# Moving the x loads to GpSimd's queue in a spectral filter with an MLP behind it, without zero fill, and with divided last stores

## The chip, the cores and the metric

The kernel runs on one core of a Trainium2 chip. The metric is the device time of one execution in microseconds (us); lower is better. Three runs of the kernel before gave a median of 1433.49 us (1433.35 to 1434.29).

A core has five engines with an instruction queue each: TensorE (PE in the profile; its weight loads are PEld), VectorE (DVE), ScalarE (ACT), GpSimd (POOL) and SyncE (SP). Transfers between the main memory and the on-chip memory are issued from the queues of SP, ACT and POOL and carried out by 16 DMA engines. Every queue works in order: an instruction that waits holds up all that stand behind it on that queue.

## What is computed

The reference, cut to what matters:

```python
X = np.fft.rfft(x, axis=1)                    # x: 4 sequences of 3008 points, 256 channels
Yr = Xr @ w_r - Xi @ w_i + b_r                # complex 256 x 256 mix of the channels
Yi = Xr @ w_i + Xi @ w_r + b_i
Yr = np.sign(Yr) * np.maximum(np.abs(Yr) - 0.01, 0.0)   # the same for Yi
y = np.fft.irfft(Y, n=x.shape[1], axis=1)
h = y.reshape(12032, 256) @ w_in              # w_in: 256 x 2048
out = (h * (1.0 / (1.0 + np.exp(-h)))) @ w_out   # w_out: 2048 x 256
```

## The kernel before

The transform of a sequence (3008 = 47 x 64 points) is a chain of four matrix stages. The first stage, s1 (L166), multiplies x by the table c1. For it a sequence is laid out in 94 rows (NP, two for each of 47) and cut into eight pieces g = 0 to 7 of 1024 columns, so one piece is 94 rows of 4 KB, 376 KB. A piece is loaded by x_load (L143), multiplied in two halves of 512 columns, copied out of PSUM by ScalarE (L184), and stored as 96 rows to a scratch tensor in main memory (L187, 384 KB). For the first sequence (b = 0), pieces 0 to 3 go through PE as plain float32 (L183); pieces 4 to 7 (S1_SPLIT) are first split on VectorE into a high and a low part (cast L179, subtraction L180) and multiplied as three float32r products (s1_product, L162 to L164). Behind the first stage the scratch is read back by pairs of residues (u_load, L229 to L233), twelve pairs u for each sequence: second stage s2 (L236), channel mix and shrinking (mix, L254), third stage i1 (L361), stored to a second scratch. The last stage (i2) runs by blocks of 512 rows and feeds the MLP (mlp1, split_g, mlp2), which runs over ticks (block, hidden slice) and takes the largest part of the time. The transforms of the later sequences are put between the MLP's ticks.

The order of the work is written out by hand (the part under `tc.manual_schedule()`, from L553); each engine and each queue follows that order. What stands around the change:

- At the start POOL clears the tile `zero` (L561) and VectorE clears rows 64 to 127 of seven x buffers (x_pre, L562 to L563). SP loads c1 as 128 rows, of which the last 34 are zeros (L564). Then x_ahead is called seven times (L565 to L566), which issues the loads of pieces 0 to 6 of the first sequence; they go on SP's queue, all other x loads on POOL's (L149). ScalarE and POOL make the high and the low part of c1 (L568, L569). PE runs warming multiplications on `zero` (L577, L578).
- Then come a load of the second stage's first table on SP (t2_load) and the first stage's loop (L643), s1(0, g) for g = 0 to 7, whose stores are issued on SP. After s1(0, 0) and s1(0, 1) another x_ahead each loads piece 7 and the second sequence's piece 0, into the buffers of pieces 0 and 1, on POOL.
- Behind the loop: two weight loads, u_load of the pairs 0, 1 and 2 and the bias on SP, the second sequence's piece 0 through the first stage, four more warming multiplications (L654), and the steps u_step(0, u) (L657), within which the MLP's weights are loaded and split, and seven more x loads are issued.
- At the very end four stores of the last 256 output rows remain: of 68, 60, 34 and 94 rows of 1 KB, by the rows of the transform's layout in which they lie. They are issued by the last loop (L755, L756), the third (k = 2) on POOL and the others on SP. The program's closing line, L776, waits for all transfers and drains the engines.

Of the kernel before, what the change touches and what calls it, by code (L numbers as in the profile page):

```python
# [16 lines left out]

# The sequence of S = 47 * 64 points, t = n1 + 64 n2, f = r + 47 k.
S, D, DFF, NB = 3008, 256, 2048, 4
RR, KK = 47, 64  # L20
NR = 24                 # residues r = 0..23; the others are their conjugates
NU = NR // 2            # pairs of residues
NJ = 32                 # n1 = 32 h + j; row 32 p + j with p = 2 n2 + h
NP = 94
# [4 lines left out]
W_PLAN = [(1, 1), (1, 1), (1, 0), (2, 1), (1, 1), (1, 0), (1, 1), (3, 1), (0, 0), (1, 0), (1, 1), (2, 0), (1, 0)]  # L29
# The first sequence's pieces that are multiplied as float32r parts.  # L30
S1_SPLIT = (4, 5, 6, 7)
# Where the first two sequences' pieces go: of seven buffers.
X_BUFS = [0, 1, 2, 3, 4, 5, 6, 0, 1, 2, 3, 4, 5, 2, 1, 0]
# [3 lines left out]
def dft_tables():  # L37
    """The transforms' tables: of the shapes alone."""
    n1 = np.arange(KK)
    n2 = np.arange(RR)  # L40
    r = np.arange(NR)
    k = np.arange(KK)

    def trig(num, den):
        num = np.mod(num, den)
        c, s = np.cos(2 * np.pi * num / den), np.sin(2 * np.pi * num / den)
        s = np.where(2 * num % den == 0, 0.0, s)
        return c, s

    # first stage: rows p = 2 n2 + h, columns m = 4 r + 2 ri + h  # L50
    c, s = trig(np.outer(n2, r), RR)
    c1 = np.zeros((RR, 2, NR, 2, 2))
    c4 = np.zeros((NR, 2, 2, RR, 2))
    for h in range(2):
        c1[:, h, :, 0, h] = c
        c1[:, h, :, 1, h] = -s
        c4[:, 0, h, :, h] = c.T
        c4[:, 1, h, :, h] = -s.T
    c1[:, :, 0, 1, :] = 0.0
    c4[0, 1] = 0.0  # L60
    # second stage, by residue: rows (ri, n1), columns (ri, k)
    f = r[:, None] + RR * k[None, :]
    flip = np.where(2 * f > S, -1.0, 1.0)
    c, s = trig(n1[None, :, None] * f[:, None, :], S)
    c2 = np.zeros((2, KK, NR, 2, KK))
    fl = flip[None, :, :]
    ct, st = c.transpose(1, 0, 2), s.transpose(1, 0, 2)
    c2[0, :, :, 0, :] = ct
    c2[1, :, :, 0, :] = st
    c2[0, :, :, 1, :] = -st * fl  # L70
    c2[1, :, :, 1, :] = ct * fl
    # and back: rows (ri, k), columns (ri, n1)
    fc = np.where(2 * f > S, S - f, f)
    wt = np.where((fc == 0) | (2 * fc == S), 1.0, 2.0) / S
    wt[0, KK // 2 + 1:] = 0.0
    c3 = np.zeros((2, KK, NR, 2, KK))
    ck, sk = c.transpose(2, 0, 1), s.transpose(2, 0, 1)
    w_, f_ = wt.T[:, :, None], flip.T[:, :, None]
    c3[0, :, :, 0, :] = w_ * ck
    c3[1, :, :, 0, :] = -w_ * f_ * sk  # L80
    c3[0, :, :, 1, :] = w_ * sk
    c3[1, :, :, 1, :] = w_ * f_ * ck
    c3[:, :, 0, 1, :] = 0.0
    c3 = c3.reshape(128, NR * 128).astype(np.float32)
    bits = c3.view(np.uint32).astype(np.uint64)
    bits = ((bits + 0x7FF + ((bits >> 12) & 1)) & 0xFFFFF000).astype(np.uint32)
    c3h = bits.view(np.float32)
    c3l = c3 - c3h
    return {
        "c1": np.pad(c1.reshape(NP, 96), ((0, 128 - NP), (0, 0))).astype(np.float32),  # L90
        "c2": c2.reshape(128, NR * 128).astype(np.float32),
        "c3": np.stack([c3h.reshape(128, NU, 256), c3l.reshape(128, NU, 256)], axis=2).reshape(128, NU * 512),
        "c4": c4.reshape(96, NP).astype(np.float32),
    }
# [3 lines left out]
def spectral_mlp_kernel(ctx: ExitStack, tc: tile.TileContext, x, w_r, w_i, b_r, b_i, w_in, w_out, c1, c2, c3, c4, out):  # L98
    nc = tc.nc
# [20 lines left out]
    def bank(name):  # L120
        """A PSUM bank for a transform; the MLP's are free before it starts."""
        tag, bufs = "d", 2
        if state["prologue"]:
            state["d"] = (state["d"] + 1) % 4
            tag, bufs = (("d", 2), ("acc", 4), ("h", 2), ("acc", 4))[state["d"]]
        return ps.tile([128, 512], F32, tag=tag, bufs=bufs, name=name)
# [3 lines left out]
    def store(dst, src, late=False):  # L130
        """A late store goes out when its data is there and what is urgent is on its way."""
        if late or not state["prologue"]:
            stores.append((dst, src))
        else:
            nc.scalar.dma_start(out=dst, in_=src)
# [5 lines left out]

    # ---- the sequence's transform, residues of the frequency first
    def x_load(b, g):  # L143
        if b < 2:
            t = x_pre[X_BUFS[8 * b + g]]
        else:
            t = x_sb[g % 2]
        v = x[b].rearrange("(p j) d -> p (j d)", j=NJ)
        (nc.sync if b == 0 and g < 7 else nc.gpsimd).dma_start(out=t[:NP, :], in_=v[:, g * 4 * D:(g + 1) * 4 * D])  # L149
        return t  # L150
# [11 lines left out]
    def s1_product(p, hl):  # L162
        for n, (m, k) in enumerate(((0, 0), (0, 1), (1, 0))):
            nc.tensor.matmul(out=p[:96, :], lhsT=c1_hl[m], rhs=hl[k], start=(n == 0), stop=(n == 2))  # L164

    def s1(b, g, late=False):  # L166
# [6 lines left out]
        for i in range(2):  # L173
            p = bank("s1")
            h = t[:, i * 512:(i + 1) * 512]
            if b == 0 and g in S1_SPLIT:
                k, w, n = ("x", 768, 2) if (2 * g + i) % 5 > 2 else ("g", 512, 3)
                hl = [sb.tile([128, w], F32R, tag=k + q, bufs=n, name="sx")[:, :512] for q in "hl"]
                nc.vector.tensor_copy(out=hl[0], in_=h)  # L179
                nc.vector.tensor_sub(hl[1], h, hl[0])  # L180
                s1_product(p, hl)
            else:
                nc.tensor.matmul(out=p[:96, :], lhsT=c1_sb, rhs=h, start=True, stop=True)  # L183
            nc.scalar.copy(o[:, i * 512:(i + 1) * 512], p[:96, :])  # L184
# [6 lines left out]
    def s1_split(b, g, i):  # L191
        t = x_t[b, g][:, i * 512:(i + 1) * 512]
        sx = sb.tile([128, 2, 512], F32R, tag="sx", bufs=1, name="sx")
        nc.scalar.copy(sx[:, 0, :], t)
        nc.vector.tensor_sub(sx[:, 1, :], t, sx[:, 0, :])
        x_t[b, g, i] = sx
# [77 lines left out]

    # The mix in three products instead of four, rows (r, f):
    # (Xr + Xi) w_r - Xi (w_r + w_i) and (Xr + Xi) w_r + Xr (w_i - w_r).
    def mix3_weights():
# [106 lines left out]
    def pieces(c0, n):  # L384
        """Runs of columns (b, j, p) in order: offset, b, j, p0, length."""
        c = c0
# [20 lines left out]
    def i2_columns(p, o, e, b, j, p0, m):  # L407
        """Row j's points p0 .. p0 + m, turned, to p's columns from o on."""
        q = (j % 4) * D + e * 128
# [4 lines left out]
    def i2(i, e):  # L414
        """Block i's rows that lie wholly in it, for one half of d."""
        c0, n = BLOCKS[i]
# [11 lines left out]
    def i2_ends(i):  # L428
        """The row that starts in the block before, which was kept, and the row that ends in the next."""
        c0, n = BLOCKS[i]  # L430
# [16 lines left out]

    # ---- the MLP
    gf = {}
# [77 lines left out]
    def w64_split(t, shape, hi, lo):  # L527
        """A float64's words (low, high) as two float32r parts. The high word times 2^-112, as a
        float32, has float32's exponent three bits too low; so moved, and with its sign, it is the
        float32 of 20 mantissa bits. The low word is scaled by that one's power of two."""  # L530
        def shaped(a):
# [21 lines left out]
    with tc.manual_schedule():  # L553
# [7 lines left out]
        nc.gpsimd.memset(zero, 0.0)  # L561
        for t in x_pre:  # L562
            nc.vector.memset(t[64:128, :], 0.0)  # L563
        nc.sync.dma_start(out=c1_sb, in_=c1)  # L564
        for _ in range(7):  # L565
            x_ahead()  # L566

        nc.scalar.copy(c1_hl[0], c1_sb)  # L568
        nc.gpsimd.tensor_sub(c1_hl[1], c1_sb, c1_hl[0])  # L569

        def warm(a, n):
            """Keeps the tensor engine's clock up while the data is on its way."""
            p = bank("warm")
# [23 lines left out]
        def w_begin():  # L597
            """A load ahead, and the first part of the next chunk that is loaded."""
            w_ahead()
# [21 lines left out]

        # steps of a batch's pairs of residues, each a pair in three places
        def u_step(b, u):
# [80 lines left out]
        def put(t, fn, *args):  # L704
            """Work for the tensor engine: at the first tick from t on that has none yet."""
            while t in taken:
# [48 lines left out]
        for k, (dst, src) in enumerate(stores):  # L755
            (nc.gpsimd if k == 2 else nc.sync).dma_start(out=dst, in_=src)  # L756

# [22 lines left out]
```

## Time and profile before

| what | value |
|---|---|
| runs: median (lowest to highest) | 1433.49 us (1433.35 to 1434.29) |
| span of the profiled execution | 1433.3 us |
| mean granted TensorE clock | 0.976 |
| PE busy | 1375.6 us (96%) |
| DVE, ACT, POOL busy | 902.6, 708.2, 165.7 us |
| moved by DMA | 105.09 MB, mean 73 GB/s |

The profile gives one execution by its span, from the first to the last instruction; no other time of that execution is recorded, and the span is 0.2 us below the median of the runs. "x4" counts instructions: one float32 multiplication of 512 columns stands as two. The slices of the page are 40 equal parts of the span, 35.8 us each, and a digit is a share in tenths. In the windows view the clock is the share of full speed that was granted to TensorE, and "DMA share" the mean busy share of the 16 DMA engines. SPq, POOLq and so on are the queues' own instructions: transfers that are issued, and waits. In the chain of waits each row is the piece of work that what follows had to wait for.

### The profile page before, as it was taken

To read this page: it belongs to the slowest core of one execution; us is meant where nothing else is said; L and a number is where in the kernel's file an instruction comes from. 1 tells how busy PE (TensorE), PEld (TensorE's weight loads), DVE (VectorE), ACT (ScalarE), POOL (GpSimd) and SP (SyncE) were. 2 spreads that over 40 slices of the span, in tenths; PEclk is the share of its full clock that TensorE was granted. 3 is DMA by queue.
4 is the path that set the end of the run, shared out by engine and by line. 5 is a ranking of instruction groups with operands and counts; after the bars stand their busy time and mean duration, and the time that the engine had idled before them with its cause. 6 is when DMAs were issued, how large, how long until landed. Compare 5 with 4: busy or idle time off the path is not lost.

```text
span 1433.3 us, 20433 instructions
## 1 busy us (share of the span) xinstructions
PE 1375.6 (96%) x7614; PEld 1171.1 (82%) x7614; DVE 902.6 (63%) x1486; ACT 708.2 (49%) x1390; POOL 165.7 (12%) x200
## 2 busy tenths in 40 slices
PE   4599899999999999999999999999999999999997
PEld 1297678888888888888888888888888888888886
DVE  1278986878665577677765566776755555555554
ACT  1256555555555445555554454554544444444444
POOL 0056541111100011110100001111100000000000
PEclk7699999999999999999999999999999999999999
DMA  1498533233143122232221221211110010001001
GB/s 66 152 298 244 174 78 104 75 103 85 41 128 95 45 63 74 81 111 63 70 75 37 70 67 41 81 54 55 38 45 26 26 38 4 24 26 38 5 11 23
DMA packets 69679, 105.09 MB, mean 73 GB/s; under 512 B 7074, under 2 KB 51201, under 8 KB 69580
## 3 DMA queue, kind: packets, MB, share of 16 engines
q1 hardware_dynamic: 56348, 77.61, 18.5%
q0 software_dynamic: 9744, 22.25, 6.1%
q10 hardware_dynamic: 3488, 3.93, 0.9%
q8 instruction: 60, 0.98, 0.3%
q14 instruction: 39, 0.32, 0.1%
HBM read 66.28 MB, written 37.49 MB: 72 GB/s over the span
## 4 chain that ended last, share of the span: by engine, by line
PE 62%; issue 28%; DMA 4%; DVE 3%; SPq 2%; ACT 1%; POOL 0%; ACTq 0%; POOLq 0%; DVEq 0%
PE h L458 23%; PE acc L487 16%; PE acc L491 8%; PE mix L324 5%; PE s L299 2%; PE i L410 2%; PE i L368 2%; DMA x_pre<-in_x_dram 2%; PE s L164 2%; SPq L149 2%; DMA scr<-i1o 1%; PE mix L263 1%; DVE ww L540 1%; DMA w<-in_moe_w_in_dram 0%; PE i2e L410 0%
## 5 line engine op out<-in xcount | busy, mean ns | idle before, releaser
L458 PE MATMUL h<-xt,win 128*128 128x512 f32 (+1 forms) x2304 | 588.1, 391 | 2.2 <-ACT xt L443 2.2
L487 PE MATMUL acc<-wout,gh 128*128 128x512 f32 x1504 | 552.4, 401 | 0.0
L458 PEld LDWEIGHTS h<-xt,win 128*128 128x128 f32 x2304 | 403.7, 189 | 86.2 <-ACT xt L443 2.4
L491 PE MATMUL acc<-wout,gl 128*128 128x256 f32 x1504 | 422.4, 281 | 5.5 <-DVE gl L474 5.5
L464 ACT ACTIVATE g<-h 128x512 f32<-128x512 f32 (+1 forms) x384 | 226.3, 589 | 387.7 <-PE h L458 383.1
L465 DVE TENSOR_TENSOR g<-h,g 128x512 f32<-128x512 f32 (+1 forms) x384 | 261.2, 680 | 241.1 <-ACT g L464 237.5
L474 DVE TENSOR_TENSOR gl<-g,gh 128x512 fp32r<-128x512 f32 (+1 forms) x384 | 283.6, 738 | 175.1 <-ACT gh L473 169.5
L487 PEld LDWEIGHTS acc<-wout,gh 128*128 128x128 f32 x1504 | 283.7, 189 | 60.1 <-ACT gh L473 0.3
L473 ACT CAST gh<-g 128x512 fp32r<-128x512 f32 (+1 forms) x384 | 235.0, 612 | 156.7 <-DVE g L465 154.3
L491 PEld LDWEIGHTS acc<-wout,gl 128*128 128x128 f32 x1504 | 284.8, 189 | 17.1 <-DVE gl L474 8.3
L331 POOL TENSOR_TENSOR q<-q,bias 128x256 f32<-128x256 f32 x36 | 26.4, 733 | 673.2 <-ACT q L330 673.2
L344 DVE TENSOR_TENSOR y<-q,mix 64x256 f32<-64x256 f32 x144 | 60.3, 419 | 2.2
L410 PEld LDWEIGHTS i<-c_sb,gin 96*128 96x128 f32 x420 | 54.4, 191 | 6.0 <-issue 1.7
L410 PE MATMUL i<-c_sb,gin 96*128 96x94 f32 x420 | 53.7, 272 | 1.2 <-DMA gin<-scr 1.2
L164 PE MATMUL s<-sx,c 128*96 128x512 f32 x120 | 38.8, 440 | 12.8 <-DVE sx L179 12.6
L368 PE MATMUL i<-zh,t 128*128 128x256 f32 x192 | 45.3, 298 | 0.0
L756 POOL DMA_DIRECT2D out_dram<-o x1 | 0.6, 550 | 378.9 <-DVE o L500 378.9
L164 PEld LDWEIGHTS s<-sx,c 128*96 128x96 f32 x120 | 21.1, 179 | 25.5 <-issue 15.8
L184 ACT COPY s1o<-s 96x512 f32<-96x512 f32 x26 | 14.4, 585 | 55.0 <-PE s L183 35.2
L299 PEld LDWEIGHTS s<-t,a 128*128 128x128 f32 x288 | 37.7, 191 | 3.0
L299 PE MATMUL s<-t,a 128*128 128x128 f32 x288 | 37.9, 274 | 0.0
L183 PE MATMUL s<-x_sb,c_sb 128*96 128x512 f32 x32 | 20.2, 775 | 15.5 <-DMA x_sb<-in_x_dram 15.5
(106 smaller groups left out, 1271.7 us busy)
## 6 DMA issues: line engine op xcount, KB each, us to landing
a<-scr SPq DMA_DIRECT2D x48, 256.0 KB
t<-in_c_dram POOLq DMA_DIRECT2D x48, 256.0 KB, 3.0
gin<-scr SPq DMA_DIRECT2D x32, 384.0 KB
scr<-s1o SPq DMA_DIRECT2D x27, 384.0 KB
scr<-i1o SPq DMA_DIRECT2D x36, 256.0 KB
x_sb<-in_x_dram POOLq DMA_DIRECT2D x22, 376.0 KB, 4.3
t<-in_c_dram SPq DMA_DIRECT2D x48, 128.0 KB
w<-in_moe_w_in_dram SPq DMA_DIRECT2D x8, 512.0 KB
```

Of the source, the lines that this page charges most:

```text
L164: nc.tensor.matmul(out=p[:96, :], lhsT=c1_hl[m], rhs=hl[k], start=(n == 0), stop=(n == 2))
L299: nc.tensor.matmul(out=pv[:, e, :, r, :], lhsT=a[:, r, e * 128:(e + 1) * 128], rhs=t2[:, r * 128:(r + 1) * 128], start=True, stop=True,)
L324: nc.tensor.matmul(out=out, lhsT=x_[:, e, c, :], rhs=m[:, e, :], start=(n == 0), stop=(n == 5))
L368: nc.tensor.matmul(out=pv[:, r, :], lhsT=t3[:, m, r * 128:(r + 1) * 128], rhs=z[:, r, :], start=(n == 0), stop=(n == 2),)
L410: nc.tensor.matmul(out=p[:, o:o + m], lhsT=g_t[b, j // 4][:, q:q + 128], rhs=c4_sb[:, p0:p0 + m], start=True, stop=True,)
L458: nc.tensor.matmul(out=p[:, :n], lhsT=w[:, e, f * 128:(f + 1) * 128], rhs=v[:, e, :n], start=(m == 0), stop=(m == 5),)
L464: nc.scalar.activation(out=g[:, :n], in_=p[:, :n], func=ACTF.Sigmoid)
L465: nc.vector.tensor_tensor(out=g[:, :n], in0=p[:, :n], in1=g[:, :n], op=ALU.mult)
L473: nc.scalar.copy(gh[:, :n], g[:, :n])
L474: nc.vector.tensor_sub(gl[:, :n], g[:, :n], gh[:, :n])
L487: nc.tensor.matmul(out=a, lhsT=gh[:, q], rhs=wout[:, f].rearrange("p a c -> p (a c)"), start=(f == 0), stop=False,)
L491: nc.tensor.matmul(out=a[:, D:2 * D], lhsT=gl[:, q], rhs=wout[:, f, 0, :], start=False, stop=(f == NFF - 1),)
```

## The change

- All x loads go on POOL's queue, the seven of the first sequence too.
- The seven x buffers are no longer cleared in rows 64 to 127. c1 has 94 rows instead of 128, and every instruction of the first stage that reads x or c1 (matmuls, casts, subtractions) takes 94 rows.
- Each of the last four stores becomes two: as many rows as make a multiple of 16, on SP for even k and on ACT for odd k, and the rest, on POOL for k = 2 and on SP otherwise. 68, 60, 34 and 94 rows become 64 + 4, 48 + 12, 32 + 2 and 80 + 14.

Comments and docstrings are dropped as well; they are left out here.

```diff
-        "c1": np.pad(c1.reshape(NP, 96), ((0, 128 - NP), (0, 0))).astype(np.float32),
+        "c1": c1.reshape(NP, 96).astype(np.float32),
...
-        (nc.sync if b == 0 and g < 7 else nc.gpsimd).dma_start(out=t[:NP, :], in_=v[:, g * 4 * D:(g + 1) * 4 * D])
+        nc.gpsimd.dma_start(out=t[:NP, :], in_=v[:, g * 4 * D:(g + 1) * 4 * D])
...
-            nc.tensor.matmul(out=p[:96, :], lhsT=c1_hl[m], rhs=hl[k], start=(n == 0), stop=(n == 2))
+            nc.tensor.matmul(out=p[:96, :], lhsT=c1_hl[m][:NP, :], rhs=hl[k][:NP, :], start=(n == 0), stop=(n == 2))
...
-            h = t[:, i * 512:(i + 1) * 512]
+            h = t[:NP, i * 512:(i + 1) * 512]
...
-                nc.vector.tensor_copy(out=hl[0], in_=h)
-                nc.vector.tensor_sub(hl[1], h, hl[0])
+                nc.vector.tensor_copy(out=hl[0][:NP, :], in_=h)
+                nc.vector.tensor_sub(hl[1][:NP, :], h, hl[0][:NP, :])
...
-                nc.tensor.matmul(out=p[:96, :], lhsT=c1_sb, rhs=h, start=True, stop=True)
+                nc.tensor.matmul(out=p[:96, :], lhsT=c1_sb[:NP, :], rhs=h, start=True, stop=True)
...
-        t = x_t[b, g][:, i * 512:(i + 1) * 512]
+        t = x_t[b, g][:NP, i * 512:(i + 1) * 512]
...
-        nc.scalar.copy(sx[:, 0, :], t)
-        nc.vector.tensor_sub(sx[:, 1, :], t, sx[:, 0, :])
+        nc.scalar.copy(sx[:NP, 0, :], t)
+        nc.vector.tensor_sub(sx[:NP, 1, :], t, sx[:NP, 0, :])
...
-        for t in x_pre:
-            nc.vector.memset(t[64:128, :], 0.0)
-        nc.sync.dma_start(out=c1_sb, in_=c1)
+        nc.sync.dma_start(out=c1_sb[:NP, :], in_=c1)
...
-        nc.scalar.copy(c1_hl[0], c1_sb)
-        nc.gpsimd.tensor_sub(c1_hl[1], c1_sb, c1_hl[0])
+        nc.scalar.copy(c1_hl[0][:NP, :], c1_sb[:NP, :])
+        nc.gpsimd.tensor_sub(c1_hl[1][:NP, :], c1_sb[:NP, :], c1_hl[0][:NP, :])
...
-            (nc.gpsimd if k == 2 else nc.sync).dma_start(out=dst, in_=src)
+            m = dst.shape[0] // 16 * 16
+            (nc.scalar if k % 2 else nc.sync).dma_start(out=dst[:m], in_=src[:m])
+            (nc.gpsimd if k == 2 else nc.sync).dma_start(out=dst[m:], in_=src[m:])
```

## The prediction

> **What bounds the kernel now.** I read the page's slices first, then the chain of waits in order of time, then the windows of the stretch that stands out. The page's first two parts:
>
> ```profile
> span 1433.3 us, 20433 instructions
> PE 1375.6 (96%) x7614; PEld 1171.1 (82%) x7614; DVE 902.6 (63%) x1486; ACT 708.2 (49%) x1390; POOL 165.7 (12%) x200
> PE   4599899999999999999999999999999999999997
> DMA  1498533233143122232221221211110010001001
> ```
>
> PE is at 9 tenths everywhere but in the first two slices (0 to 72 us) and the last. So PE bounds the run after about 72 us, and before that something else does. The DMA row says that it isn't the sixteen engines as a whole: they are at 1 and 4 tenths there. The chain of waits up to 72 us names it:
>
> ```profile
> 7.47 0.92 DVE x_pre L563
> 8.39 4.57 SPq L149
> ...
> 13.01 8.75 SPq L149
> 21.80 8.66 SPq L149
> 30.51 27.84 DMA x_pre<-in_x_dram
> 58.95 5.00 PE s L164 x12
> 63.97 0.59 ACT s1o L184
> 64.58 4.07 DMA scr<-s1o
> 68.66 2.63 DMA a<-scr
> 71.43 1.15 PE s L242 x8
> ```
>
> From 13 to 58 us the chain is nothing but loads of x from SP's queue, one piece every 8.7 us or so. Then the last split pieces are multiplied, the last one is stored, pair 0 is read back, and the second stage starts at 71.43. The windows view shows how the loads run (columns: stretch, length, busy time of PE, PEld, DVE, ACT, POOL with counts, granted clock, DMA share, GB/s):
>
> ```profile
> 5.26:8.67 3.41, 0.10 (x1) 0.00 (x0) 2.74 (x3) 0.00 (x0) 0.00 (x0) 0.96 0.12 50
> 32.57:35.98 3.41, 0.00 (x0) 0.00 (x0) 0.00 (x0) 0.01 (x1) 0.00 (x0) 0.96 0.13 53
> 17.70:18.70 1.00, 0.00 (x0) 0.00 (x0) 0.00 (x0) 0.00 (x0) 0.00 (x0) 0.98 0.81 262
> 49.00:50.00 1.00, 0.00 (x0) 0.00 (x0) 0.00 (x0) 0.00 (x0) 0.00 (x0) 0.50 0.98 320
> 66.70:70.11 3.41, 2.38 (x6) 0.76 (x4) 0.11 (x1) 0.71 (x2) 0.00 (x0) 1.00 0.63 202
> 70.11:73.52 3.41, 1.43 (x9) 1.29 (x10) 0.60 (x2) 1.40 (x3) 2.35 (x3) 0.96 0.74 238
> 73.52:76.94 3.42, 3.42 (x18) 3.42 (x18) 1.37 (x2) 1.33 (x4) 0.00 (x0) 0.54 1.01 300
> ```
>
> A share of 0.12 to 0.13 at 50 to 53 GB/s is two of sixteen engines at full pace. In the window 17.70 to 18.70 a load of the same shape from POOL's queue is under way beside it, and the share is 0.81 at 262 GB/s. So the same 94 rows go over two engines from SP and over nearly all from POOL. The Trainium skill's page "DMA: Bandwidth & Descriptors", section "Why a DMA increments its semaphore by 16 and not by 1", gives a reason: a transfer takes the largest number of engines up to 16 that divides its slowest dimension, which for 94 is 2, and some direct copies from GpSimd are excepted and take all 16. The trace agrees, with 0.13 against 0.81.
>
> **The change, part by part.** The instructions that carry the sum, from the timeline, and POOL's fourteen x loads after 200 us (least, median and most to landing), from the view of that tile. The last two lines are the transfers' sizes:
>
> ```profile
> 0.78 0.53 POOL L561 MEMSET zero<- 128x512 f32 x1
> 1.36 4.00 PE L575 MATMUL warm<-zero 128*128 128x512 f32 x6 [1.36 <-POOL zero L561]
> 2.56 0.27 ACT L568 CAST c<-c_sb 128x96 fp32r<-128x96 f32 x1 [0.32 <-DMA c_sb<-in_c_dram]
> 19.82 3.70 PE L183 MATMUL s<-x_sb,c_sb 128*96 128x512 f32 x4 [4.59 <-DMA x_sb<-in_x_dram]
> 58.37 0.43 DVE L179 CAST sx<-x_pre 128x512 fp32r<-128x512 f32 x1 [4.97 <-DMA x_pre<-in_x_dram]
> 60.51 0.42 DVE L179 CAST sx<-x_sb 128x512 fp32r<-128x512 f32 x1
> 62.02 0.69 DVE L180 TENSOR_TENSOR sx<-x_sb,sx 128x512 fp32r<-128x512 f32 x1
> 63.77 1.88 PE L183 MATMUL s<-x_sb,c_sb 128*96 128x512 f32 x4
> 71.94 1.13 POOL L219 DMA_DIRECT2D t<-in_c_dram  x2
> L149 POOL DMA_DIRECT2D x_sb<-in_x_dram x14: 516/552/553, 291.3 to 721.6; - x14
> DMA to landing us min/median/max: 3.4/3.9/6.8
> x_sb<-in_x_dram POOLq DMA_DIRECT2D x22, 376.0 KB, 4.3
> scr<-s1o SPq DMA_DIRECT2D x27, 384.0 KB
> ```
>
> *Loads moved to POOL.* The seven loads are queued behind POOL's memset of zero, which ends at 1.31. One issue takes 0.57 us (1.13 for two), so the seventh is out by 5.3. What stands behind them on POOL is the low part of c1 and then the load of piece 7, which waits for the multiplication of piece 0 anyway, so the issue time is covered. Piece 0 lands at 1.31 + 3.9 = 5.2. After that the loads follow one another at the rate that all engines give: 376 KB are 385,000 bytes, at 300 GB/s (window 73.52 to 76.94) 1.28 us. A store of the first stage, 384 KB, takes 1.31 by the same rate.
>
> *Zero fill gone.* The seven memsets on VectorE, the last of which ends at 8.39 and stands in the chain, held SP's issues of x and nothing else: VectorE's next work is the cast of piece 4. With them kept, POOL's loads would have waited for them; without them the loads can start at 1.31. No row shows a matmul over 94 contracted rows. I see no reason for a loss; 94/128 of 1.88 would be 0.5 less a piece, but what is late next is the landing of pieces 4 and 7 (below), so this gains nothing either way. The later sequences' casts and subtractions over 94 partitions are off PE's path and are taken as unchanged.
>
> *c1 with 94 rows.* The load of c1 stays on SP, and I take it to go over two engines like x. Its landing is bounded by 2.5 us (now, row of the cast at 2.56) and by what x's 94 rows take from SP, 8.7 after the issue, so at most 9.5. A row of it is 384 bytes against 4,096, a tenth, so I take 3.5, hidden behind piece 0's landing at 5.2. At the upper end it costs 4 us.
>
> *PE in the first stage.* The warming matmuls end at 5.36. Four unsplit pieces at full clock (1.88) end at 5.4 + 7.5 = 12.9; at half clock (3.70) they would end at 20.2. I take full clock: the windows show that PE keeps the clock after a window with 2.38 busy of 3.41, and loses it after one with 1.43; pieces every 1.28 us keep PE busy from 5.4 on.
>
> *Split pieces.* VectorE needs 60.51 - 58.37 = 2.14 for a piece. Piece 4 lands at 5.2 + 4 x 1.28, and a store beside it, 11.6; four pieces end at 20.2 if none is late. Piece 7 can be late: by its landing the engines have moved eight loads and about four stores from 3.9 on, 8 x 1.28 + 4 x 1.31 = 15.5, so 19.4. VectorE then ends at 19.4 + 2.14 = 21.6, and I take this. The last product ended 63.95 - 62.71 = 1.24 after the last subtraction: 22.8.
>
> *To the second stage.* Copy, store, reading back: 71.43 - 63.97 = 7.46, all DMA trips that the change doesn't touch. Second stage at 22.8 + 7.5 = 30.3 instead of 71.43: **41.1 us earlier**. From there on every instruction and every transfer is issued in the order and at the distances of before. So the whole of the rest moves.
>
> *Last stores.* The end, from the timeline, SP's waits after 1400 us and the instructions of the closing line:
>
> ```profile
> 1424.46 0.96 SPq L756 DMA_DIRECT2D out_dram<-o  x3
> 1425.08 0.55 POOL L756 DMA_DIRECT2D out_dram<-o  x1 [378.88 <-DVE o L500]
> SPq L776 <- DMA out_dram<-o: 3.5, 2, 2.4
> SPq L776 <- PEq L776: 3.5, 2, 3.0
> L776 POOLq DRAIN x3: 46/102/7514, 1425.0 to 1433.1; - x3
> ```
>
> Four stores become eight: SP gets five issues for three (2 x 0.32 more), ACT two, POOL keeps one, of two rows. The store of 94 rows, over two engines, lands last now and is what SP waits 2.4 us for. Split, its 80 rows are a multiple of 16 like the first stage's stores of 96 rows, which ran at a share of 0.98 (window 49 to 50, when nothing but such stores and a load of x was on its way), so those 2.4 shrink to well under 1. But then SP waits 3.0 more, and POOL's drain, 7.5 us from 1425.05, ends just then, at 1432.56. If the drain has a fixed length, nothing is gained; if it ends 3 us after POOL's own store has landed, some 2.2 are. Nothing here tells the two apart; I take **1.0**, the middle, and keep 0 and 2.2.
>
> The sum: 1433.3 - 41.1 - 1.0 = 1391.2 against the profiled execution's span; the median of the runs, 1433.49, is 0.2 above it, so the forecast is **1391.4**.
>
> **The rivals.**
>
> *Loads from POOL one at a time.* If its queue starts a load only when the one before has landed, piece 7 lands at 1.3 + 8 x 3.9 = 32.5, the second stage starts at 32.5 + 2.1 + 1.2 + 7.5 = 43.3, and the time is 1433.5 - 28.1 - 1.0 = 1404.4. For it: seven loads in a row on POOL do not occur in the trace. Against: two issues in 1.13 us show no wait between them, where one load takes 3.9 to land.
>
> *Left-over transfers.* The DMA row is at 9 and 8 tenths from 72 to 143 us. If three stores or loads slip past the start of the second stage, that crowded stretch takes 3 x 1.3 more: about 1395. Against: in the chain the reading back follows the landing of the last store, and the others go out ahead of it on the same queue.
>
> *POOL's loads on two engines as well*, the side that is slower. Then seven pieces take as long as now, and piece 7, which POOL loads today early, stands behind them on the same two engines: 94 rows at about 8.2 us a piece end it some 7.5 us after piece 6's 58.4, at 65.9 instead of before 60.5, so the second stage is 5 us later and the time 1438. It decides from the point where a piece takes longer than today's 8.2 to 8.7 us. Against: the share of 0.81 at 17.70. The same skill page, section "Issuing engines are not separate DMA queues", speaks against the change: issuing from another engine only saves sequencer time, since all transfers run on the same engines. That rule leads to this rival, with its time and its chance; the trace differs, with 262 GB/s from POOL and SP together against 50 from SP.
>
> **How the numbers follow.** A measurement of this kernel can tell about 0.2% (2.9 us) from no change. Chances: the forecast 0.82, left-over transfers 0.07, one at a time 0.07, two engines 0.04. The forecast's own bounds: piece 0 at 1.31 + 3.4, no store in the way, 1.5 us less on an emptier DMA at the stage's end and 2.2 at the tail give 1385, and a clock window falling well 1 more, 1384; half clock through the unsplit pieces (7.3) and a c1 at its upper end give about 1402. So 1384 to 1402, which holds left-over transfers too and leaves out the other two and a little. Faster 0.95, within 0.2% 0.01, slower 0.04.
>
> **What would show it.** In the profile after: DMA share above 0.7 from 3 us on; x's loads all POOLq; DVE's first cast at 10 to 13 us; the first matmul of L242's line at 28 to 33 us; granted clock full from 5 us through the first stage; the u-steps after it of the same length; the drain of POOL either near 7.5 us or shorter. It would be wrong if the first x piece landed after 8 us, if pieces came further apart than 2 us, if the clock fell to half in the unsplit pieces, or if the stretch from the second stage's start to the end grew beyond 1362 us, which it has now.

## The result, and the profile after

The changed kernel takes 1399.31 us (median of four runs, 1399.06 to 1402.53) against 1433.42 for the kernel before (1432.9 to 1434.29). The ratio is 0.9768, with a 95% interval of 0.9754 to 0.9782: 34 us are gained where 42 were forecast. The page of the profile after, its first parts:

```profile
span 1397.4 us, 20421 instructions
...
PE   9998999999999999999999999999999999999997
...
PEclk6998999999999999999999999999999999999999
DMA  7985332322323214242121121220210110011001
```

PE is now at 8 or 9 tenths from the first slice on, and DMA at 7 in the first slice instead of 1: the two slices at the start in which PE stood at 4 and 5 are gone. But the granted clock is 6 tenths in the first slice, over which PE is at 9. The chain of waits says what this is worth:

```profile
1.34 6.29 DMA x_sb<-in_x_dram
...
7.67 12.76 PE s L183 x16
20.42 10.24 PE s L164 x24
30.66 3.41 PE s L183 x4
34.08 4.57 PE warm L573 x8
38.65 0.91 PE s L242 x8
```

Where loads of x stood from 13 to 58 us, PE itself now stands from 7.67 to the second stage. The second stage (L242) starts at 38.5 instead of 71.43, which is 32.9 us. From there to the end of the span it is 1358.9 us, against 1361.9 before. The windows of the first stage in the profile after (stretch, length, busy time of PE, PEld, DVE, ACT, POOL, granted clock, DMA share, GB/s):

```profile
5.57:8.93 3.36, 1.26 (x3) 0.57 (x4) 0.00 (x0) 0.13 (x1) 0.00 (x0) 1.00 1.04 244
8.93:12.34 3.41, 3.41 (x5) 1.11 (x4) 0.00 (x0) 1.45 (x3) 0.54 (x1) 0.50 1.02 239
32.82:36.24 3.42, 3.42 (x5) 1.35 (x4) 0.27 (x1) 1.69 (x4) 0.00 (x0) 0.50 0.84 264
36.24:39.65 3.41, 3.41 (x17) 2.11 (x16) 0.42 (x1) 0.41 (x2) 2.35 (x3) 1.00 0.77 218
```

PE waits for the first piece until 7.67, loses the clock at 8.93, and then works without a gap for 27 us at half clock. It gets the clock back only at 36.24, behind the window in which the second set of warming multiplications, over 128 rows, begins (at 33.87). Before the change a single piece over 128 rows at half clock was enough to bring it back (0.96 in the window 32.57 to 35.98 of the prediction, behind the piece that ended there). So the question is what holds the clock down, and whether it was the idle time alone.

The end, in the profile after: the timeline, SP's waits and the closing line.

```profile
1388.29 0.77 DVE L500 TENSOR_TENSOR o<-acc,o 128x256 f32<-128x256 f32 x2 [0.88 <-ACT o L499]
1389.36 0.54 POOL L756 DMA_DIRECT2D out_dram<-o  x1 [378.89 <-DVE o L500]
SPq L776 <- PEq L776: 4.7, 2, 4.2
SPq L776 <- DMA out_dram<-o: 1.0, 1, 1.0
L776 POOLq DRAIN x3: 46/102/7249, 1389.3 to 1397.1; - x3
```

In SP's waits the last number is the longest one. It is 1.0 us for stores instead of 2.4, and then 4.2 instead of 3.0 for other queues. The line puts that down to PE's queue; by the drain's row, the queue that is late is POOL's, whose drain still takes 7.2 us. From VectorE's last instruction to the end it is 8.3 us, 8.5 before.

### The profile page after: what moved, and what is told of

Same layout as the page of the kernel before. It is cut to its first block, busy times and chain, and to the rows that moved or that the text cites. A ratio compares the mean times of both kernels' runs of the same rounds, so it can differ in the third digit from the quotient of the medians.

```text
span 1397.4 us, 20421 instructions
## 1 busy us (share of the span) xinstructions
PE 1374.6 (98%) x7614; PEld 1172.3 (84%) x7614; DVE 894.1 (64%) x1479; ACT 708.7 (51%) x1390; POOL 171.3 (12%) x207
## 4 chain that ended last, share of the span: by engine, by line
PE 64%; issue 29%; DVE 3%; DMA 2%; ACT 1%; POOL 1%; ACTq 0%; SPq 0%; POOLq 0%; DVEq 0%
PE h L458 23%; PE acc L487 16%; PE acc L491 8%; PE mix L324 5%; PE s L164 2%; PE s L299 2%; PE i L410 2%; PE i L368 2%; PE s L183 1%; DMA w<-in_moe_w_in_dram 1%; DMA scr<-i1o 1%; PE mix L263 1%; DVE ww L540 1%; DVE gl L474 1%; PE i2e L410 0%
## 5 line engine op out<-in xcount | busy, mean ns | idle before, releaser
L331 POOL TENSOR_TENSOR q<-q,bias 128x256 f32<-128x256 f32 x36 | 26.3, 732 | 672.4 <-ACT q L330 672.4
L164 PE MATMUL s<-sx,c 94*96 94x512 f32 x120 | 39.1, 450 | 0.3 <-DVE sx L195 0.3
L368 PEld LDWEIGHTS i<-zh,t 128*128 128x128 f32 x192 | 33.1, 190 | 0.9 <-issue 0.3
L500 DVE TENSOR_TENSOR o<-acc,o 128x256 f32<-128x256 f32 x94 | 33.2, 415 | 0.9 <-ACT o L499 0.9
L332 POOL TENSOR_TENSOR q<-q,bias 128x256 f32<-128x256 f32 x36 | 32.3, 897 | 2.8
```

The source lines that it names most:

```text
L164: nc.tensor.matmul(out=p[:96, :], lhsT=c1_hl[m][:NP, :], rhs=hl[k][:NP, :], start=(n == 0), stop=(n == 2))
L368: nc.tensor.matmul(out=pv[:, r, :], lhsT=t3[:, m, r * 128:(r + 1) * 128], rhs=z[:, r, :], start=(n == 0), stop=(n == 2),)
```

## The experiments

**The rows back at 128.** Loads and last stores stay as changed; c1 is padded and the buffers are cleared again:

```diff
-            h = t[:NP, i * 512:(i + 1) * 512]
+            h = t[:, i * 512:(i + 1) * 512]
...
-        nc.sync.dma_start(out=c1_sb[:NP, :], in_=c1)
+        for t in x_pre:
+            nc.vector.memset(t[64:128, :], 0.0)
+        nc.sync.dma_start(out=c1_sb, in_=c1)
```

> The changed kernel with the first stage back at 128 rows: c1 padded, the x buffers cleared in rows 64 to 127 again, all x loads still on POOL. Theory: PE's half clock from 9 to 36 us comes from contracting only 94 rows, which does not count as full activity. Then the clock is full from about 12 to 16 us on, the second stage starts at about 32 instead of 38.5, and the time is near 1393. Rival: the clock was lost only because PE idled from 5.6 to 7.7, and nothing in the first stage could bring it back; then it stays at half until about 36 us and the time is 1399 to 1400.

Measured: 1391.37 us (1391.03 to 1392.47), 7.9 us less than the change. PE's instructions from the timeline:

```profile
6.40 5.36 PE L183 MATMUL s<-x_sb,c_sb 128*96 128x512 f32 x12 [0.84 <-DVE x_pre L563]
28.74 1.23 PE L242 MATMUL s<-t,a 128*128 128x128 f32 x8 [2.01 <-DMA a<-scr]
```

Three plain pieces take 5.36 us, all at full clock, and the second stage starts at 28.7. The time is on the side of the theory of the rows, but in this profile the clock was never lost in the first stage, so it does not yet show that 128 rows bring it back. Nor does the run change the rows alone. The clears space the loads: POOL issues the first at 2.24 and each further one about 1.1 us later, PE begins at 6.40 instead of 7.67, and it idles for 0.84 us ahead of the first piece instead of 2.10.

**A longer warming.** Five multiplications of zeros instead of two, 94 rows kept:

```diff
-        warm(zero, 2)
+        warm(zero, 5)
```

> The changed kernel with five warming multiplications of 512 columns instead of two, so that PE is busy from 1.4 until the first piece has landed. Theory of the rows: the clock is full until the warming is over, and falls to half within one or two windows of 3.4 us once only 94-row multiplications run; the time falls by 1.5 to 3.5 to about 1396 to 1398. Rival (the idle gap alone): full clock through the whole first stage, second stage at about 31, time near 1392.

Measured: 1392.27 us (1391.04 to 1393.08), the rival's number.

```profile
1.36 7.22 PE L573 MATMUL warm<-zero 128*128 128x512 f32 x12 [1.36 <-POOL zero L561]
8.42 5.32 PE L183 MATMUL s<-x_sb,c_sb 94*96 94x512 f32 x12
14.89 7.34 PE L164 MATMUL s<-sx,c 94*96 94x512 f32 x24
```

With the gap closed, 94 rows run at full clock through the stage. The theory that 94 rows make PE lose the clock falls here. The edit does two things: it closes the gap, and it keeps PE busy for 7.22 us, some two steps of the clock's record (3.41 us each), so that one whole window is busy nearly wherever the steps fall.

**Rows without a gap.** Extra multiplications of zeros, stretch after stretch with other rows and columns, so that this kernel does more than the reference asks; its time says nothing:

```diff
+        def probe(k, m, n):
+            p = bank("probe")
+            for _ in range(n):
+                nc.tensor.matmul(out=p[:m, :], lhsT=zero[:k, :m], rhs=zero[:k, :], start=True, stop=True)
+
+        for k, m, n in ((128, 128, 16), (94, 96, 16), (128, 96, 16), (94, 96, 16), (128, 128, 16),
+                        (94, 128, 16), (128, 128, 16), (64, 96, 16), (128, 128, 16), (128, 64, 16)):
+            probe(k, m, n)
```

> The changed kernel with 160 extra float32 multiplications of 512 columns of zeros ahead of the first stage, without a gap, in stretches of 16: (rows contracted, columns of the weight) 128x128, 94x96, 128x96, 94x96, 128x128, 94x128, 128x128, 64x96, 128x128, 128x64. Theory of the rows: granted clock 1.0 in the 128-row stretches, 0.5 in those of 94 and 64 rows within two windows of 3.4 us, whatever the columns; a stretch takes about 14 us at full and 27 at half clock. Rival: full clock in all, since PE never idles, some 14 us for each stretch.

Measured: all ten stretches in 138.8 us, at full clock throughout (one window over all of them):

```profile
4.10:142.90 138.80, 138.80 (x322) 55.66 (x320) 5.22 (x10) 0.00 (x0) 1.35 (x3) 1.00 0.07 17
```

Once the clock is full, even 64 rows keep it through a stretch of some 14 us. The theory, as it stood, is wrong; what is left open is whether few rows can raise the clock.

**Rows after a gap.** The same, but PE waits before every stretch for twelve copies of ScalarE, and so starts each at half clock:

```diff
+        def probe(k, m, n):
+            for _ in range(12):
+                nc.scalar.copy(gap, zero)
+            p = bank("probe")
+            for _ in range(n):
+                nc.tensor.matmul(out=p[:m, :], lhsT=gap[:k, :m], rhs=gap[:k, :], start=True, stop=True)
```

> The changed kernel with nine extra stretches of 12 float32 multiplications of 512 columns of zeros ahead of the first stage; before each, PE waits for twelve copies of ScalarE (some 7 us), so that it starts each at half clock. Stretches (rows contracted, columns of the weight): 128x128, 94x96, 128x96, 94x128, 112x96, 104x96, 96x96, 64x128, 128x64. A stretch takes 20.4 us if the clock stays at half and 12 to 15 if it comes back after one or two windows of 3.4 us. Theory (94 rows keep a full clock, as the stretches without a gap showed, but cannot bring it back): 128 rows come back, 94, 96 and 64 do not, with the limit somewhere between 96 and 128. Rival: the rows do not matter and all come back; then the half clock from 9 to 36 us in the changed kernel has another cause.

The stretches one by one, in the order of the expectation (128x128, 94x96, 128x96, 94x128, 112x96, 104x96, 96x96, 64x128, 128x64):

```profile
11.44:24.07 12.63, 12.63 (x24) 5.27 (x24) 5.21 (x10) 0.00 (x0) 0.00 (x0) 0.83 0.22 54
31.98:52.78 20.80, 20.80 (x24) 6.62 (x24) 0.00 (x0) 0.00 (x0) 0.00 (x0) 0.50 0.00 0
60.69:74.27 13.58, 13.58 (x24) 4.74 (x24) 0.00 (x0) 0.00 (x0) 0.00 (x0) 0.77 0.00 0
82.17:103.02 20.85, 20.85 (x24) 7.92 (x24) 0.00 (x0) 0.00 (x0) 0.00 (x0) 0.50 0.00 1
110.92:123.28 12.36, 12.36 (x24) 4.43 (x24) 0.00 (x0) 0.00 (x0) 0.00 (x0) 0.85 0.00 0
131.19:143.66 12.47, 12.47 (x24) 4.46 (x24) 0.00 (x0) 0.00 (x0) 0.00 (x0) 0.84 0.00 0
151.56:164.08 12.52, 12.52 (x24) 4.46 (x24) 0.00 (x0) 0.00 (x0) 0.00 (x0) 0.84 0.00 0
171.99:192.83 20.84, 20.84 (x24) 7.82 (x24) 0.00 (x0) 0.00 (x0) 0.00 (x0) 0.50 0.00 0
200.74:214.24 13.50, 13.50 (x25) 3.92 (x25) 0.00 (x0) 0.00 (x0) 0.00 (x0) 0.78 0.00 0
```

With 128, 112, 104 and 96 contracted rows the clock comes back within the stretch (0.77 to 0.85 on the mean, 12.4 to 13.6 us). With 94 and 64 rows it stays at 0.50 for the whole 20.8 us, though PE has no gap. The columns don't matter: 128x64 comes back, 94x128 doesn't. The theory is right in that 94 and 64 rows don't bring the clock back, and missed with 96 rows, which do. The Trainium skill, page "TensorE: Matmul & The Clock Gate", Part 1, states that the halved clock is the default and that a busy window of about 3.4 us releases it. The clock's records here do step in such windows (3.41 us); but windows that are busy from end to end with 94 or 64 rows don't release it here, and of the counts tried 96 is the smallest that does.

**POOL without a store at the end.**

```diff
-            (nc.gpsimd if k == 2 else nc.sync).dma_start(out=dst[m:], in_=src[m:])
+            nc.sync.dma_start(out=dst[m:], in_=src[m:])
```

> The changed kernel with the last store of two rows on SP instead of POOL, so that POOL issues nothing at the end. Theory: POOL's drain lasts 7.2 to 7.5 us from its own last store, whatever the rows; without that store the end comes about 1 us after SP's last landing, 3 to 4 us earlier, about 1395.5. Rival: the drain waits for all transfers or has that length anyway; then no change beyond 0.5 us.

Measured: 1387.84, 1394.74, 1396.82 and 1388.11 us, median 1391.42. Two things happened in one. The end: SP's waits and the closing line,

```profile
SPq L776 <- DMA out_dram<-o: 1.0, 2, 0.5
...
SPq L776 <- PEq L776: 0.7, 2, 0.5
L776 POOLq DRAIN x3: 51/102/7386, 1002.2 to 1385.8; - x3
```

show POOL's drain at its old length, but begun at 1002 us, with POOL's last work, and the wait of 4.2 us down to 0.5. That is worth some 4 us. And the times fall into two groups 7 to 9 us apart; the theory's 1395.5 is that of the upper one. The profiled execution, of 1387.84, is one in which the first stage kept the clock: its windows show 1.00 where the change's show 0.50, though PE idled too, for 1.49 us instead of 2.10. First the timeline's row, then two windows:

```profile
6.74 5.39 PE L183 MATMUL s<-x_sb,c_sb 94*96 94x512 f32 x12 [1.49 <-DMA x_sb<-in_x_dram]
```

```profile
4.79:8.20 3.41, 1.92 (x7) 0.76 (x5) 0.00 (x0) 0.32 (x1) 0.68 (x2) 1.00 1.05 273
9.00:13.00 4.00, 4.00 (x11) 1.60 (x10) 0.14 (x1) 2.64 (x5) 1.05 (x2) 1.00 1.02 251
```

So whether the clock is lost depends on the execution. The steps of the clock's record fall differently too: the record of this trace begins at 4.79, so that the next step is at 8.20, that of the change's at 5.52 and 8.93. The window here holds 1.92 us of PE's work and the clock is kept; the change's holds 1.26 and it is lost, as behind the 1.43 of the window 70.11 to 73.52 in the prediction.

**The change once more**, unaltered:

> The changed kernel itself, looked at again, since the end of PE's idle time ahead of the first piece was 7.6 us in its profile and 6.7 us in that of the kernel with its last store on SP, whose first stage kept the full clock. Theory: the landing of the first piece varies by over 1 us between executions, and with it whether the clock is lost; the times then fall into groups some 7 us apart, about 1391 and 1399. Rival: the half clock belongs to this kernel in every execution, all times within 1398 to 1403.

Measured: 1400.37, 1399.27, 1400.09 and 1401.53 us, so the rival's single group, and the theory of two groups missed for this kernel. In this profile the first three pieces take 10.55 us, half clock from the start:

```profile
7.42 10.55 PE L183 MATMUL s<-x_sb,c_sb 94*96 94x512 f32 x12 [1.85 <-DMA x_sb<-in_x_dram]
```

The clock's record of this trace begins only at 37.16, when the clock comes back. Ahead of it the views print 1.00, but the multiplications take 1.06 us each instead of 0.59, and that is half clock. So in this execution the clock was not lost in the gap: it had not come up by the first piece. Counted back from 37.16 in steps of 3.41, no window up to 9.85 is busy throughout (3.03 to 6.44 has 2.54 us of work), and from there to the second warming, at 34.84, PE runs 94 rows only. Both profiled executions of the change ran the first stage at half clock, by two different ways, and the eight times (1399.06 to 1402.53) are alike. That the place of the steps decides is a reading of three profiles and no more. Why the kernel with the store moved at the end escaped in two of four executions, and the change in none of eight, stays open; the two are the same up to the last stores.

**The first loads on SP, as 80 and 14 rows.**

```diff
-        nc.gpsimd.dma_start(out=t[:NP, :], in_=v[:, g * 4 * D:(g + 1) * 4 * D])
+        for q in (slice(0, 80), slice(80, NP)) if b == 0 and g < 7 else (slice(0, NP),):
+            (nc.sync if b == 0 and g < 7 else nc.gpsimd).dma_start(out=t[q, :], in_=v[q, g * 4 * D:(g + 1) * 4 * D])
```

> The changed kernel with the seven first loads back on SP, each as 80 and 14 rows instead of 94; 94 rows in the first stage as in the change. Theory: what the move to POOL bought is the number of DMA engines, not the queue; then the pieces land at about 1.3 us apart from SP too, the first at 4 to 5, PE never loses the clock, and the time is 1389 to 1392. Rival: SP's queue itself is slow; then a piece takes 4 us or more and the time is above 1405.

Measured: 1392.04 us (1389.98 to 1392.85).

```profile
5.36 5.39 PE L184 MATMUL s<-x_sb,c_sb 94*96 94x512 f32 x12
10.59 1.88 PE L184 MATMUL s<-x_pre,c_sb 94*96 94x512 f32 x4
```

PE goes on from its warming without a gap, at full clock. So SP's queue is not slow; what was slow before the change is a transfer of 94 rows in one piece, which SP sent over two engines. POOL helped because its 94 rows went over nearly all engines. By the Trainium skill's page "DMA: Bandwidth & Descriptors", section "Issuing engines are not separate DMA queues", all transfers run on the same engines, whichever queue issues them. The run agrees: with the rows divided, SP is as fast as POOL (1392.04 us, and 1392.27 with POOL and five warming multiplications).

Later in this profile the clock is lost after all, at 19.09, in the split pieces, and it comes back at 25.92:

```profile
25.49 3.81 PE L574 MATMUL warm<-zero 128*128 128x512 f32 x8
22.50:25.92 3.42, 3.42 (x5) 1.22 (x4) 0.00 (x0) 1.17 (x3) 0.00 (x0) 0.50 1.00 299
25.92:29.33 3.41, 3.38 (x8) 1.14 (x6) 0.44 (x1) 1.45 (x3) 0.00 (x0) 1.00 0.59 181
```

The window that brings it back holds 94 rows up to 25.49 and only 0.43 us of warming over 128 rows. So 34 rows more for an eighth of the window were enough. An estimate of the mean over this window, from 2.99 us of 94 rows and 0.43 us of 128, is 98 rows.

**The rows alone**, on the kernel before the change: 94 rows, no zero fill, loads and last stores as before. Against the changed kernel:

```diff
-        nc.gpsimd.dma_start(out=t[:NP, :], in_=v[:, g * 4 * D:(g + 1) * 4 * D])
+        (nc.sync if b == 0 and g < 7 else nc.gpsimd).dma_start(out=t[:NP, :], in_=v[:, g * 4 * D:(g + 1) * 4 * D])
...
-            m = dst.shape[0] // 16 * 16
-            (nc.scalar if k % 2 else nc.sync).dma_start(out=dst[:m], in_=src[:m])
-            (nc.gpsimd if k == 2 else nc.sync).dma_start(out=dst[m:], in_=src[m:])
+            (nc.gpsimd if k == 2 else nc.sync).dma_start(out=dst, in_=src)
```

> The rows alone: the kernel before the change with 94 rows and no zero fill in the first stage, all loads and the last stores as before. The stage is bound by loads on two engines, so by the theory the half clock hides behind them up to the last pieces; only pieces 6 and 7, the second sequence's first piece and the warming are late, by 1 to 4 us, against at most 1 us that the loads start earlier: 1433 to 1437. If the 94 rows cost their 7 to 8 us whatever bounds the stage, 1441.

Measured: 1433.91 us, ratio 1.0 (0.999 to 1.0009). From its timeline:

```profile
64.54 3.62 PE L183 MATMUL s<-x_sb,c_sb 94*96 94x512 f32 x4
72.52 2.02 PE L242 MATMUL s<-t,a 128*128 128x128 f32 x16
```

The last piece takes 3.62 instead of 1.88, and the second stage starts 1.1 us later. As long as the loads bound the stage, the half clock was all but free; it became a price only when the loads had been made fast.

The same stretch shows the rows at work on the kernel's own data. The first two windows are those of the kernel before, with 128 rows, the last two those of this run, with 94:

```profile
59.87:63.29 3.42, 3.42 (x9) 2.16 (x9) 2.75 (x5) 2.88 (x7) 0.00 (x0) 0.54 0.54 171
63.29:66.70 3.41, 3.41 (x10) 1.57 (x9) 0.00 (x0) 2.32 (x4) 0.00 (x0) 1.00 0.98 291
59.99:63.40 3.41, 3.41 (x9) 2.17 (x9) 2.77 (x6) 2.91 (x6) 0.00 (x0) 0.50 0.51 163
63.40:66.82 3.42, 3.42 (x7) 1.54 (x6) 0.00 (x0) 1.45 (x3) 0.00 (x0) 0.50 0.86 264
```

One gapless window with 128 rows brings the clock back; with 94 rows two of them don't.

**The divided last stores alone**, on the kernel before the change:

```diff
-            (nc.gpsimd if k == 2 else nc.sync).dma_start(out=dst, in_=src)
+            m = dst.shape[0] // 16 * 16
+            (nc.scalar if k % 2 else nc.sync).dma_start(out=dst[:m], in_=src[:m])
+            (nc.gpsimd if k == 2 else nc.sync).dma_start(out=dst[m:], in_=src[m:])
```

> The divided last stores alone: the kernel before the change with only its last four stores changed, POOL still with its store of two rows. Theory (POOL's drain of 7.2 to 7.5 us behind its own store sets the end): 0.2 to 0.5 us faster, not to be told from no change. Rival (the end follows SP's last landing): 2 us faster, 1432.

Measured: 1433.19 us, ratio 0.9995 (0.9986 to 1.0004), so no change that can be told. In SP's waits and the closing line, here L778, the end hangs on POOL's drain again:

```profile
SPq L778 <- PEq L778: 4.5, 2, 4.0
SPq L778 <- DMA out_dram<-o: 0.3, 1, 0.3
L778 POOLq DRAIN x3: 46/93/6679, 1423.6 to 1430.7; - x3
```

**The parts that help, together.** 128 rows, loads on POOL, no POOL store at the end. This is the edit of the first experiment and that of the end together:

```diff
-            h = t[:NP, i * 512:(i + 1) * 512]
+            h = t[:, i * 512:(i + 1) * 512]
...
-            (nc.gpsimd if k == 2 else nc.sync).dma_start(out=dst[m:], in_=src[m:])
+            nc.sync.dma_start(out=dst[m:], in_=src[m:])
```

> The changed kernel with 128 rows and zero fill in the first stage as before the change, loads on POOL, and no POOL store at the end. If the gain of the 128 rows (8 us) and that of the end (about 4 us by the traces) are independent, 1387 to 1388. If a rival is right by which both only hit the fast half of two kinds of execution, its times spread like those of the kernel with its last store on SP (1388 to 1397).

Measured: 1387.74 us (1387.57 to 1388.24), ratio to the kernel before 0.9678 (0.9662 to 0.9694). The gains add: without POOL's store it is 3.6 us less than the first experiment's 1391.37. And the times no longer fall into groups.

The same end with 94 rows and five warming multiplications:

```diff
-        warm(zero, 2)
+        warm(zero, 5)
...
-            (nc.gpsimd if k == 2 else nc.sync).dma_start(out=dst[m:], in_=src[m:])
+            nc.sync.dma_start(out=dst[m:], in_=src[m:])
```

> The changed kernel with five warming multiplications and no POOL store at the end: 94 rows, no zero fill. If the clock once full is kept by 94 rows and the two gains add, as those of the 128 rows and the end did, 1387.5 to 1389 in every execution. If keeping depends on the phase of the clock's windows, single executions at 1394 to 1397.

Measured: 1388.67 us (1388.32 to 1389.1), all four in the lower group.

The same end with 96 rows; c1 is padded to 96 rows and the buffers are cleared in rows 64 to 95. One of the lines:

```diff
-                nc.tensor.matmul(out=p[:96, :], lhsT=c1_sb[:NP, :], rhs=h, start=True, stop=True)
+                nc.tensor.matmul(out=p[:96, :], lhsT=c1_sb[:96, :], rhs=h, start=True, stop=True)
```

> As the kernel with 128 rows and no POOL store at the end, but with 96 rows: c1 padded to 96, the x buffers cleared in rows 64 to 95. Theory (96 rows bring the clock back, 94 don't): 1387 to 1388.5, like 128 rows. Rival (the limit found with zeros does not hold for the first stage's data and weights): the clock is lost in most executions and the time is 1394 to 1397.

Measured: 1387.92 us (1387.16 to 1389.14). Its profile shows the clock come back inside the first stage, on the kernel's own data:

```profile
6.54 7.53 PE L183 MATMUL s<-x_sb,c_sb 96*96 96x512 f32 x12 [0.97 <-DVE x_pre L563]
13.90 1.88 PE L183 MATMUL s<-x_pre,c_sb 96*96 96x512 f32 x4
```

Three pieces take 7.53 us, between 5.3 (full clock) and 10.5 (half), and the next one 1.88. The change's 94 rows, without a gap from 8.93 on, had not done this in 27 us. With the stretches behind a gap above, two rows more than 94 decide it.

## Why the forecast held in its direction and missed in its size

*The bound named was right.* Loads on two engines bound the first stage, and moving them freed it: with 128 rows kept, the second stage starts at 28.7, against 30.3 forecast.

*The loads* came at the rate of all engines, but later than in the sum: the first landed at 7.6 instead of 5.2, and VectorE's first cast came at 13.94 instead of 11.6 (timeline of the profile after):

```profile
3.46 0.27 ACT L566 CAST c<-c_sb 94x96 fp32r<-94x96 f32 x1 [1.22 <-DMA c_sb<-in_c_dram]
13.94 0.42 DVE L179 CAST sx<-x_pre 94x512 fp32r<-94x512 f32 x1 [13.94 <-DMA x_pre<-in_x_dram]
```

The landing of 3.9 was that of a load by itself; with seven issued in a row the first took 6.3. Dropping the clears had a price here: issued one by one behind them, in the run with the rows back at 128, the loads start 0.9 us later and the first is there by 6.4. None waited for another's landing (the rival at 1404), and none went over two engines (the slower side). c1 was ready at 3.46, as forecast (3.5).

*The step that failed* is PE in the first stage: "I take full clock", and with it, of 94 rows, "I see no reason for a loss". The first half went wrong because PE idled for 2.1 us ahead of the first piece, where the sum had it go on from the warming (in the second profile of the change the warming had not raised the clock at all). The second half is the larger error: with 128 or 96 rows the clock comes back within a window or two; with 94 it did not, for 27 us. Runs with the rows at 128 (and the shorter gap that the clears bring), and with the gap closed, take 7.9 and 7.0 us off the change. The prediction had named half clock in the unsplit pieces as a sign of being wrong; the first cast at 13.94 and the second stage at 38.5 lie outside what it named as well.

*The range.* It held the time, 1399.3, but in part by luck. Its upper end, 1402, is made of 7.3 us for half clock in the unsplit pieces and up to 4 for a late c1, and c1 cost nothing. By the sum's own terms the unsplit pieces at half clock end at 20.2, ahead of VectorE's 21.6; with full clock behind them, less than 7.3 would have reached the second stage. The 8.2 us measured there came about because the half clock lasted through the split pieces (11.23 us against 7.34 with five warming multiplications) and the second sequence's piece (3.62 against 1.88) too.

*To the second stage.* 7.46 was taken for the DMA trips. Measured are 7.8 from the last product of the first stage, but the trips were hidden: what stood on the path was the second sequence's piece (3.4), at half clock, and the warming (4.6), at half clock up to 36.24.

*The rest* was forecast to move as a block, and was 3.0 us shorter. Some 1.7 of it can be the window 73.52 to 76.94 of before, which ran at a clock of 0.54 right behind the second stage's start and has no counterpart. Matched one by one, PE's instructions lie 32.9 us earlier at the second stage's start, 34.7 at the first mixing multiplication, 35.9 from 243 us of before on and 35.7 at the end; what makes up the remaining 1.0 to 1.2 ahead of 243 us stays open. Left-over transfers would have made it longer, so that rival falls.

*The end* was given 1.0, between 0 and 2.2; it gave 0.2 in the trace, and alone, in the run with the divided stores only, 0.8, which can't be told from nothing. Of the two cases that the sum left open, the runs show the first: POOL's drain took 6.7 to 7.5 us from POOL's last instruction on, wherever that lay, and was hidden where POOL had nothing to do late.

*Span and time.* The forecast added 0.2 to the span. Each execution's time turned out to lie 1.7 to 1.8 us over its span (1399.14 for 1397.4); so the profiled execution of before, with its span of 1433.3, was by this a longer one (about 1435) than the three that were shown with it. In spans, 1391.2 was forecast and 1397.4 measured: 8.2 too late at the second stage, less 2.0 for the rest and the end together.

## What to carry to other kernels

Before cutting rows that "only multiply zeros", ask whether the engine's clock depends on them: here PE with 94 contracted rows at half clock stayed there, and with 96 it did not. When a wait is removed, the engine that takes over is priced at the clock that it has in the new timeline, and a gap of 2 us at the start cost 7 here. And ask over how many engines a transfer of a given row count goes: here 80 and 14 rows from SP did what moving 94 rows to POOL's queue does.

## What the runs showed of the hardware that was not expected

- The granted clock, once full, is kept by gapless multiplications over 64 or 94 rows (138.8 us without a dip, in stretches of some 14), but in stretches that begin at half clock it came back with 96 rows and more (12.4 to 13.6 us for twelve multiplications) and not with 94 or 64 (20.8). The number of columns made no difference between 64 and 128. A window with 94 rows and 0.43 us of 128 rows was enough.
- A record of the clock can begin late: in the second profile of the change the views print 1.00 where multiplications of 1.06 us instead of 0.59 show half clock.
- POOL's drain at the program's end lasted 6.7 to 7.5 us wherever it began: at 1425.0 and 1389.3 with a last store, at 1002 without one. A store of two rows on POOL at the end cost 3.6 us (1391.37 against 1387.74, and 1392.27 against 1388.67).
- A load of 376 KB from POOL took 3.9 us to land by itself (median) and 6.3 as the first of seven issued in a row.
